# Weight loads moved to ScalarE's queue, a conversion and three copies moved in the start-up, and identity products added between its transposes

## The chip, the cores and the metric

One core of a Trainium2 chip runs the whole kernel. The metric is the device time of one execution in microseconds (us). The engines are TensorE (PE; its weight loads are PEld), VectorE (DVE), ScalarE (ACT), GpSimd (POOL) and SyncE (SP), whose queue issues DMA transfers.

## The reference

```python
def _attn_ref(q, k, v):                      # (4, 8, 576, 64), float32
    scores = scale * np.matmul(q, k.transpose(0, 1, 3, 2))
    rel = pos[:, None] - pos[None, :]
    mask = (rel >= 0) & (rel < 64)
    scores = np.where(mask, scores, -1000000000.0)
    attn = softmax(scores)                   # max taken off, sum + 1e-9
    return np.matmul(attn, v)

def _moe_ref(x, w_gate, w_val, w_out, rms_g):   # (2304, 512), d_ff 1536
    xn = x / sqrt(mean(x * x) + 1e-06) * rms_g
    g = xn @ w_gate
    silu = g * (1.0 / (1.0 + np.exp(-g)))
    return silu * (xn @ w_val) @ w_out

def _moe2_ref(x, w_in, w_out):               # d_ff 2048
    h = x @ w_in
    return (h * (1.0 / (1.0 + np.exp(-1.702 * h)))) @ w_out
```

The three run one after the other. The weights come as 64-bit floats.

## The kernel before

The 2304 tokens are cut into tiles of 128 (index `m`) and blocks of three tiles (384 tokens, index `j`). Attention makes a tile of x from q, k and v; the first MLP goes over all blocks twice (`ps_i`), with six of its twelve slices `f` of 128 columns each time; the second MLP goes over all blocks once.

**Weights.** A pair is two slices of 512 KB, for instance gate and value of one `f`, or two slices of `w_out`; `w_order` lists 34 pairs, and the first block needs pairs 0 to 8 (0: gate and value of slice 0; 1: of slice 1; 2: output of slices 0 and 1; and so on in threes). `w_load` issues a pair's two transfers on SP's queue into one of three `st` buffers. `w_step` converts: two ScalarE operations on `st` (L144, L145), then three VectorE operations that leave a 24-bit value in `m` (L146, L147, L150), of which there is one buffer. `w_half`, called at the start of the next step, casts the high part on ScalarE (L128) and takes the rest on VectorE (L129); from then on products may use the pair. An `st` buffer is free again after L150, and the load of pair i+3 goes into the buffer of pair i.

**Start-up** (tiles 0 to 2, `starting[0]`). For each tile: transposes of k and q, S (L271), masking with a row maximum (L289), exponentials (L301), scaling by the reciprocal sum (L311 to L313), all of it for two halves `e` of four heads. The p of each half is transposed by four TensorE operations into a bank ps_t (L321) and copied to SBUF (`to_sbuf`, L233); then PV (L336), a copy to `xraw` (L344), squares (L353), sums by products with ones (L367), a power on POOL, a product that spreads it (L373), and the scaling of x by it and by `g_sb` (L377). `split_x` casts x to `xh` (L385, L387) and takes `xl` (L389). The products of the first block (`proj`, L396) start there.

**Order.** The program names engines and queues; a scheduler that ranks instructions by a simulated timeline orders each engine's instructions, and each engine and each queue then works strictly in its order, waiting on semaphores. `tc.issue_after(x)` ranks what follows behind instruction x. `hold[0]` is such an instruction for the conversions L144 and L145: in the start-up the last exponential, then the last cast of `split_x`. Attention for later blocks and the conversions are spread over slots (three per `f`) of the MLP blocks; in block 0 there is a `w_step` in every second slot, in the others of that pass one in nine.

Of the kernel before, what the change touches and what calls it, by code (L numbers as in the profile page):

```python
# [8 lines left out]
F32 = mybir.dt.float32  # L9
# [13 lines left out]
def window_attention__gated_mlp__mlp_kernel(  # L23
# [13 lines left out]
    nc = tc.nc  # L37
# [8 lines left out]
    NHP = H // 2  # L46
# [5 lines left out]
    T0 = TB  # L52
# [7 lines left out]
    acc_p = ctx.enter_context(tc.tile_pool(name="acc", bufs=1, space=PSUM))  # L60
# [6 lines left out]
    ident = const.tile([128, 128], F32, name="ident")  # L67
# [5 lines left out]
    QT0 = at.tile([128, NHP, 128], F32, name="QT")  # L73
# [25 lines left out]
    w_next = [0, 0]  # L99
# [3 lines left out]
    def w_src(kind, f):  # L103
        c = slice(f * 128, (f + 1) * 128)
        if kind in "gvh":
            w = {"g": w_gate, "v": w_val, "h": w_in2}[kind]
            return w[:, c].bitcast(I32).rearrange("(k p) f -> p k f", p=128)
        return {"o": w_out, "p": w_out2}[kind][c, :].bitcast(I32)

    def w_load(limit):  # L110
        while w_next[0] < min(limit, n_w):
            pair = w_order[w_next[0]]
            w_next[0] += 1
            st = stp.tile([128, 2, 1024], I32, tag="st", name="st")
            for e, (kind, f) in enumerate(pair):
                dst = st[:, e, :].rearrange("p (k f) -> p k f", k=KC) if kind in "gvh" else st[:, e, :]
                nc.sync.dma_start(out=dst, in_=w_src(kind, f))
            staged.append(st)

    def after(ins):  # L120
        return tc.issue_after(ins) if ins is not None else nullcontext()

    def w_half():
        if not half:
            return
        pair, w24 = half.pop()
        w = wp.tile([128, 2, 1024], F32R, tag="w", name="w")
        nc.scalar.copy(w[:, 0, :], w24.bitcast(F32))  # L128
        nc.vector.tensor_tensor(w[:, 1, :], w24.bitcast(F32), w[:, 0, :].bitcast(F32), ALU.subtract)  # L129
        for e, key in enumerate(pair):  # L130
            weights[key] = w[:, :, e * 512:(e + 1) * 512]

    def w_step(limit):
        w_half()
        if w_next[1] >= min(limit, n_w):
            return
        w_load(w_next[1] + 1)
        pair = w_order[w_next[1]]
        w_next[1] += 1
        st = staged.pop(0).rearrange("p e (f two) -> p (e f) two", two=2)  # L140
        lo, hi = st[:, :, 0], st[:, :, 1]
        m = tmp.tile([128, 1024], I32, tag="tmp", name="m")
        with after(hold[0]):
            nc.scalar.mul(hi.bitcast(F32), hi.bitcast(F32), 2.0 ** -112)  # L144
            nc.scalar.activation(lo, lo.bitcast(U32), AF.Copy, scale=2.0 ** -29)  # L145
        nc.vector.tensor_scalar(m.bitcast(U32), hi.bitcast(U32), 3, None, ALU.logical_shift_left)  # L146
        nc.vector.scalar_tensor_tensor(  # L147
            m.bitcast(U32), hi.bitcast(U32), 0x80000000, m.bitcast(U32), ALU.bitwise_and, ALU.bitwise_or
        )
        nc.vector.tensor_tensor(m, m, lo, ALU.add)  # L150
        half.append((pair, m))
        w_load(w_next[1] + 2)


    NLD = 4
# [57 lines left out]
    hold = [None]  # L213
    starting = [True]
    ps_turn = {}

    def att_bank(kind):
        shape = [128, 512]
        if not starting[0]:
            return atp.tile(shape, F32, tag="att", name="ps_" + kind)  # L220
        ps_turn[kind] = i = ps_turn.get(kind, -1) + 1
        if kind in "kq":
            return acc_p.tile(shape, F32, tag="acc" + "23"[kind == "q"], name="ps_" + kind)
        if kind == "r":
            return acc_p.tile(shape, F32, tag="acc" + "012"[i % 3], name="ps_" + kind)
        if kind == "s":
            return acc_p.tile(shape, F32, tag="acc" + "01"[i % 2], name="ps_" + kind)
        if kind == "v":
            return mm_p.tile(shape, F32, tag="gv"[i % 2], name="ps_" + kind)
        return atp.tile(shape, F32, tag="att", name="ps_" + kind)  # L230

    def to_sbuf(dst, src):
        nc.scalar.copy(dst, src)  # L233

    def att_Tk(m):
        t = ld_tile["k", m]
# [17 lines left out]
        released(("q", m))  # L254

    p_tiles = {}
    last_exp = [None]
    last_pt = [None]
    pt_tiles = {}

    def key_blocks(n):
        return slice(0, 4, 3) if n % 4 == 0 else slice((n - 1) % 4, (n - 1) % 4 + 2)

    def att_S(m):
        QT = qts[m]
        banks = [att_bank("s") for _ in range(2)]
        prev = last_pt[0] if not starting[0] else None
        for hp in range(NHP):
            for g, e in ((0, 0), (0, 1), (1, 0), (1, 1)):
                with after(prev):  # L270
                    prev = nc.tensor.matmul(  # L271
                        banks[e][64 * g:64 * g + 64, hp * 128:(hp + 1) * 128],
                        QT[64 * e:64 * e + 64, hp, 64 * g:64 * g + 64],
                        KT[64 * e:64 * e + 64, hp, key_blocks(2 * m + g), :],
                        start=True,
                        stop=True,
                    ).ins
        first = next((g for g in range(2) if (2 * m + g) % GPB == 0), None)
        mask = masks[:, MASKS.index(((m + 1) % 2, first))].rearrange("p a b -> p (a b)")
        sm = at.tile([128, 3, 2 * NHP], F32, tag="sm", name="sm", bufs=6)  # L280
        if starting[0] and m > 0:
            p = [part_tile().rearrange("p (h t) -> p h t", h=NHP) for _ in range(2)]
        else:
            pp = at.tile([128, 2 * NHP, 128], F32, tag="p", name="p", bufs=1)
            p = [pp[:, e * NHP:(e + 1) * NHP, :] for e in range(2)]
        for e in range(2):
            for hp in range(NHP):
                i = e * NHP + hp
                nc.vector.tensor_tensor_reduce(  # L289
                    p[e][:, hp, :],  # L290
                    banks[e][:, hp * 128:(hp + 1) * 128],
                    mask,
                    op0=ALU.add,
                    op1=ALU.min,
                    scale=-0.125,
                    scalar=3e38,
                    accum_out=sm[:, 0, i:i + 1],
                )
            for hp in range(NHP):
                i = e * NHP + hp  # L300
                last_exp[0] = nc.scalar.activation(  # L301
                    p[e][:, hp, :],
                    p[e][:, hp, :],
                    AF.Exp,
                    bias=sm[:, 0, i:i + 1],
                    scale=-1.0,
                    accum_out=sm[:, 1, i:i + 1],
                ).ins
        for lo, n, pe in [(0, NHP, p[0]), (NHP, NHP, p[1])] if starting[0] else [(0, 2 * NHP, pp)]:
            r = sm[:, 2, lo:lo + n]  # L310
            nc.vector.tensor_scalar(r, sm[:, 1, lo:lo + n], SUM_EPS, None, ALU.add)  # L311
            nc.vector.reciprocal(r, r)
            nc.vector.tensor_tensor(pe, pe, r.unsqueeze(2).to_broadcast([128, n, 128]), ALU.mult)  # L313
        p_tiles[m] = p

    def att_PT(m):
        for e in range(2):
            p = p_tiles[m][e]
            ps = att_bank("t")
            for hp in range(NHP):  # L320
                last_pt[0] = nc.tensor.transpose(ps[:, hp * 128:(hp + 1) * 128], p[:, hp, :], ident).ins  # L321
            if starting[0] and m > 0:
                pt = part_tile().rearrange("p (h t) -> p h t", h=NHP)
            else:
                pt = at.tile([128, NHP, 128], F32, tag="pt", name="pt", bufs=2)
            to_sbuf(pt, ps.rearrange("p (h t) -> p h t", h=NHP))
            pt_tiles[m, e] = pt

    def att_PV(m, x, c0):
# [116 lines left out]
    m = TB // 128  # L446
    for fn in (att_Tk, att_Tq):
        at_slot(0, 0, lambda m=m, fn=fn: held(fn, m))
    for b in range(1, NB):
        for i in range(TB // 128):  # L450
            m = b * TB // 128 + i
# [6 lines left out]
            h = b - 1  # L458
# [12 lines left out]
    if True:  # L471
# [1 line left out]
        nc.sync.dma_start(out=g_sb, in_=rms_g.rearrange("(k p) -> p k", p=128))  # L473
        make_identity(nc, ident)
        nc.vector.memset(QT0, 0.0)
        ps_warm = att_bank("v")
        for _ in range(10):
            nc.tensor.matmul(ps_warm[:, 0:128], QT0[:, 0, :], QT0[:, 0, :], start=True, stop=True)
        nc.vector.memset(KT[:, :, 3, :], 0.0)
        nc.vector.memset(ones, 1.0 / DM)  # L480
        nc.vector.memset(mhalf, -0.5)
# [20 lines left out]
        for m in range(T0 // 128):  # L502
            att_S(m)
            if m + 1 < T0 // 128:
                att_Tk(m + 1)
                att_Tq(m + 1)
        hold[0] = last_exp[0]
        w_step(1)
        for m in range(T0 // 128):
            att_PT(m)  # L510
            att_PV(m, x, m * 128)
            s4 = rms_sq(x, m * 128, sq)
            pe_hold = rms_scale(x, sq, m * 128, (m + 1) * 128, s4)
# [181 lines left out]
```

## Time and profile before

| | |
|---|---|
| median of 3 runs | 1029.68 us (1028.36 to 1031.18) |
| profiled execution | 1027.21 us, span 1025.4 us from first to last instruction |
| mean granted TensorE clock | 0.979 of full |
| busy, share of the span | PE 96%, PEld 89%, DVE 50%, ACT 40%, POOL 1% |
| chain that ended last | PE 83%, DVE 6%, ACT 5%, DMA 4% |

Times in the rows below count from the start of the span. A busy share is an average over the whole span; the table by stages in the rows tells the stages apart. A line L128 is line 128 of the kernel. A trace counts most 32-bit products as two records, since TensorE takes them in two passes; a transpose is one.

### The profile page before, as it was taken

The numbers are of one execution on the slowest core, as the hardware profiler recorded it, in microseconds if no ns is written. First come the engines' busy times: TensorE is split into PE (matmuls) and PEld (weight loads), VectorE is DVE, ScalarE is ACT, GpSimd is POOL, SyncE is SP. The second block draws the span as 40 slices with busy tenths as digits, with TensorE's granted clock in tenths as the row PEclk, the third lists the DMA queues.
The fourth block names the chain that finished last, engine by engine and source line by source line (L and its number), as shares of the span: only waits on it lengthen the run. The fifth ranks groups of instructions, "written<-read, shape, count | busy, mean of one in ns | idle before, by whom it ended". The sixth has DMA issues, their size and how long they took to land.

```text
span 1025.4 us, 15454 instructions
## 1 busy us (share of the span) xinstructions
PE 987.4 (96%) x6158; PEld 917.1 (89%) x6158; DVE 517.4 (50%) x1132; ACT 408.7 (40%) x884; POOL 12.2 (1%) x39
## 2 busy tenths in 40 slices
PE   7888999999989999999999999999999999999997
PEld 5877798988989899999999998998989989999996
DVE  5597756655575655656543688332232322322222
ACT  7586654654554333333332365222222222322222
POOL 2000000000000000000000000000000000000000
PEclk9698999999999999999999999999999999999999
DMA  9648644444361512423411352010010000000000
GB/s 233 184 124 212 181 102 133 101 86 135 83 186 42 196 66 87 165 72 122 157 72 63 113 171 77 1 62 1 1 62 1 32 31 1 31 1 1 32 1 31
DMA packets 113320, 88.43 MB, mean 86 GB/s; under 512 B 77664, under 2 KB 104288, under 8 KB 113248
## 3 DMA queue, kind: packets, MB, share of 16 engines
q1 hardware_dynamic: 113248, 87.44, 29.4%
q8 instruction: 48, 0.79, 0.3%
q14 instruction: 24, 0.20, 0.1%
HBM read 68.55 MB, written 18.87 MB: 85 GB/s over the span
## 4 chain that ended last, share of the span: by engine, by line
PE 83%; DVE 6%; ACT 5%; DMA 4%; issue 1%; SPq 0%; POOL 0%; DVEq 0%; ACTq 0%
PE acc L622 20%; PE psh L396 19%; PE acc L531 13%; PE psg L396 12%; PE psv L396 12%; PE ps_s L271 2%; PE ps_v L336 2%; ACT p L301 1%; PE ps_t L321 1%; DMA st<-in_moe_w_in_dram 1%; DMA st<-in_moe_w_val_dram 1%; DVE xraw L377 1%; ACT st L145 1%; DMA o<-x2s 1%; PE ps_r L367 1%
## 5 line engine op out<-in xcount | busy, mean ns | idle before, releaser
L638 DVE TENSOR_TENSOR a<-a,psh 128x384 f32<-128x384 f32 x96 | 53.0, 553 | 201.9 <-ACT a L637 201.9
L396 PE MATMUL psh<-x2h,w 128*128 128x384 f32 x768 | 153.3, 339 | 0.9 <-DVE a L638 0.6
L622 PE MATMUL acc<-w,gh 128*128 128x512 f32 x576 | 152.9, 397 | 0.0
L396 PEld LDWEIGHTS psh<-x2h,w 128*128 128x128 f32 x768 | 137.2, 188 | 4.3 <-DVE a L638 0.9
L637 ACT ACTIVATE a<-psh 128x384 f32<-128x384 f32 x96 | 47.0, 491 | 220.4 <-PE psh L396 217.2
L622 PEld LDWEIGHTS acc<-w,gh 128*128 128x128 f32 x576 | 107.1, 188 | 18.5
L531 PE MATMUL acc<-ah,w 128*128 128x384 f32 x576 | 117.6, 344 | 3.6 <-ACT w L128 3.3
L531 PEld LDWEIGHTS acc<-ah,w 128*128 128x128 f32 x576 | 103.5, 190 | 4.9 <-ACT w L128 3.7
L565 DVE SCALAR_TENSOR_TENSOR a<-a,psg 128x384 f32<-128x384 f32 x72 | 39.7, 552 | 115.5 <-ACT a L562 115.3
L396 PE MATMUL psh<-x2l,w 128*128 128x384 f32 x384 | 86.2, 338 | 0.0
L622 PE MATMUL acc<-w,gl 128*128 128x512 f32 x288 | 85.1, 396 | 0.0
L642 DVE TENSOR_TENSOR gl<-a,gh 128x384 fp32r<-128x384 f32 x96 | 53.4, 557 | 50.5 <-ACT gh L641 42.7
L562 ACT ACTIVATE a<-psg 128x384 f32<-128x384 f32 x72 | 35.1, 487 | 107.7 <-PE psg L396 107.7
L396 PEld LDWEIGHTS psh<-x2l,w 128*128 128x128 f32 x384 | 69.9, 188 | 5.9
L641 ACT CAST gh<-a 128x384 fp32r<-128x384 f32 x96 | 49.3, 513 | 62.5 <-DVE a L638 49.7
L396 PE MATMUL psg<-xh,w 128*128 128x384 f32 x288 | 65.3, 357 | 6.4 <-DVE a L565 2.6
L622 PEld LDWEIGHTS acc<-w,gl 128*128 128x128 f32 x288 | 54.2, 189 | 12.5
L531 PE MATMUL acc<-al,w 128*128 128x384 f32 x288 | 64.8, 343 | 0.0
L572 ACT CAST ah<-a 128x384 fp32r<-128x384 f32 x72 | 36.8, 511 | 70.1 <-DVE a L569 69.9
L396 PE MATMUL psv<-xh,w 128*128 128x384 f32 x288 | 62.9, 346 | 0.0
L396 PEld LDWEIGHTS psg<-xh,w 128*128 128x128 f32 x288 | 51.3, 193 | 11.4 <-DVE a L565 3.6
L301 ACT ACTIVATE p<-p,sm 128x128 f32<-128x128 f32 x128 | 49.6, 391 | 23.6 <-DVE sm L289 23.6
(104 smaller groups left out, 1433.6 us busy)
## 6 DMA issues: line engine op xcount, KB each, us to landing
st<-in_moe_w_out_dram SPq DMA_DIRECT2D x28, 512.0 KB, 4.3
o<-x2s SPq DMA_DIRECT2D x48, 192.0 KB, 3.4
st<-in_moe_w_in_dram SPq DMA_DIRECT2D x16, 512.0 KB, 5.0
st<-in_moe_w_gate_dram SPq DMA_DIRECT2D x12, 512.0 KB, 4.9
st<-in_moe_w_val_dram SPq DMA_DIRECT2D x12, 512.0 KB, 5.6
qkv<-in_v_dram SPq DMA_DIRECT2D x20, 256.0 KB, 4.2
x<-xraw SPq DMA_DIRECT2D x6, 768.0 KB, 4.7
xr<-x SPq DMA_DIRECT2D x6, 768.0 KB, 4.4
```

What stands on the lines that cost most here:

```text
L271: prev = nc.tensor.matmul(banks[e][64 * g:64 * g + 64, hp * 128:(hp + 1) * 128], QT[64 * e:64 * e + 64, hp, 64 * g:64 * g + 64], KT[64 * e ...
L301: last_exp[0] = nc.scalar.activation(p[e][:, hp, :], p[e][:, hp, :], AF.Exp, bias=sm[:, 0, i:i + 1], scale=-1.0, accum_out=sm[:, 1, i:i + ...
L396: nc.tensor.matmul(ps[:, :T], w[:, wi, c * 128:(c + 1) * 128], xx[:, c, :T], start=(i == 0), stop=(i == 3 * KC - 1),)
L531: nc.tensor.matmul(acc[c][:, :T], w[:, wi, c * 128:(c + 1) * 128], aa, start=(f == f_lo and pi == 0), stop=(f == f_hi - 1 and pi == 2),)
L562: tanh = nc.scalar.activation(a, psg[:, :T], AF.Tanh, scale=0.5).ins
L565: nc.vector.scalar_tensor_tensor(a, a, 1.0, psg[:, :T], ALU.add, ALU.mult)
L572: nc.scalar.copy(ah, a)
L622: nc.tensor.matmul(acc[c], (gh, gh, gl)[pi][:, c * 128:(c + 1) * 128], w[:, (0, 1, 0)[pi], :], start=(f == 0 and pi == 0), stop=(f == NF2 ...
L637: nc.scalar.activation(a[:, :T], psh[:, :T], AF.Sigmoid, scale=1.702)
L638: nc.vector.tensor_tensor(a[:, :T], a[:, :T], psh[:, :T], ALU.mult)
L641: nc.scalar.copy(gh[:, :T], a[:, :T])
L642: nc.vector.tensor_tensor(gl[:, :T], a[:, :T], gh[:, :T].bitcast(F32), ALU.subtract)
```

## The change

Five edits. (1) Every load of a pair behind the first three (31 pairs, 62 transfers) is issued on ScalarE's queue behind the cast L128 of the pair three before it, no longer on SP's. (2) The first `w_step`, which converts pair 0, is called behind the transposes of the last start-up tile, and its conversions are ranked behind the copy of that tile's first p half. (3) In the start-up the copy of each second p half runs on VectorE. (4) Behind each group of four p transposes in the start-up come five products of the identity with itself into a bank `ps_warm` that nothing reads. (5) A bank is renamed.

```diff
-    def w_load(limit):
+    def w_load(limit, queue=None):
+        queue = queue or nc.sync
         while w_next[0] < min(limit, n_w):
...
-                nc.sync.dma_start(out=dst, in_=w_src(kind, f))
+                queue.dma_start(out=dst, in_=w_src(kind, f))
             staged.append(st)
...
         w = wp.tile([128, 2, 1024], F32R, tag="w", name="w")
-        nc.scalar.copy(w[:, 0, :], w24.bitcast(F32))
+        cast = nc.scalar.copy(w[:, 0, :], w24.bitcast(F32)).ins
+        with tc.issue_after(cast):
+            w_load(w_next[0] + 1, nc.scalar)
...
         if w_next[1] >= min(limit, n_w):
             return
-        w_load(w_next[1] + 1)
...
         half.append((pair, m))
-        w_load(w_next[1] + 2)
...
-    def to_sbuf(dst, src):
-        nc.scalar.copy(dst, src)
+    def to_sbuf(dst, src, other=False):
+        if other:
+            return nc.vector.tensor_copy(dst, src)
+        return nc.scalar.copy(dst, src)
...
                 last_pt[0] = nc.tensor.transpose(ps[:, hp * 128:(hp + 1) * 128], p[:, hp, :], ident).ins
+            if starting[0]:
+                with tc.issue_after(last_pt[0]):
+                    for _ in range(5):
+                        nc.tensor.matmul(ps_warm[0][:, 0:128], ident, ident, start=True, stop=True)
...
-            to_sbuf(pt, ps.rearrange("p (h t) -> p h t", h=NHP))
+            copy = to_sbuf(pt, ps.rearrange("p (h t) -> p h t", h=NHP), starting[0] and e == 1)
+            if e == 0:
+                last_copy[0] = copy.ins
             pt_tiles[m, e] = pt
...
-        hold[0] = last_exp[0]
-        w_step(1)
+        ps_warm = [acc_p.tile([128, 512], F32, tag="acc3", name="ps_warm")]
         for m in range(T0 // 128):
             att_PT(m)
+            if m == T0 // 128 - 1:
+                hold[0] = last_copy[0]
+                w_step(1)
             att_PV(m, x, m * 128)
```

What the scheduler makes of it, at three places. First ScalarE in the start-up, from the exponentials of tile 1 on; `pt` and `quad<-ps_t` are copies of p halves, `st` the conversions of pair 0, `xraw` a tile of x. Before:

```order
L301 ACTIVATE quad,sm<-quad,sm 128x128 x8
L233 COPY pt<-ps_t 128x512
L301 ACTIVATE quad,sm<-quad,sm 128x128 x4
L233 COPY quad<-ps_t 128x512
L301 ACTIVATE quad,sm<-quad,sm 128x128 x3
L144 ACTIVATE st<-st 128x1024
L145 ACTIVATE st<-st 128x1024
L344 COPY xraw<-ps_v 128x4x128
L233 COPY quad<-ps_t 128x512 x2
L353 ACTIVATE s_417<-xraw 128x512
L128 CAST w<-m 128x1024
```

With the change (line numbers are the changed kernel's; L146 and L147 are the two conversions there, L129 the cast, L118 the loads):

```order
L304 ACTIVATE quad,sm<-quad,sm 128x128 x15
L236 COPY quad<-ps_t 128x512
L353 COPY xraw<-ps_v 128x4x128
L362 ACTIVATE s_422<-xraw 128x512
L236 COPY quad<-ps_t 128x512
L146 ACTIVATE st<-st 128x1024
L147 ACTIVATE st<-st 128x1024
L353 COPY xraw<-ps_v 128x4x128
L362 ACTIVATE s_478<-xraw 128x512
L129 CAST w<-m 128x1024
L118 DMA st<-in_moe_w_gate_dram 128x4x256
L118 DMA st<-in_moe_w_val_dram 128x4x256
```

The exponentials stand together, three copies are gone, the conversions have moved behind tile 0's squares and tile 2's first copy, and pair 3's transfers stand behind the cast.

Second TensorE in the same stretch, from the second half of tile 0's transposes on (`ps_r<-ones` are tile sums). Before:

```order
L321 MATMUL ps_t<-ident,p 128x128 x4
L321 MATMUL ps_t<-ident,quad 128x128 x4
L336 MATMUL ps_v<-pt,quad 64x64 x15
L321 MATMUL ps_t<-ident,quad 128x128 x4
L336 MATMUL ps_v<-quad 64x64
L321 MATMUL ps_t<-ident,quad 128x128 x4
L336 MATMUL ps_v<-quad 64x64 x15
L321 MATMUL ps_t<-ident,quad 128x128 x4
L336 MATMUL ps_v<-quad 64x64
L367 MATMUL ps_r<-ones,s_417 128x1 x4
```

With the change:

```order
L324 MATMUL ps_t<-ident,p 128x128 x4
L328 MATMUL ps_warm<-ident 128x128 x5
L324 MATMUL ps_t<-ident,quad 128x128 x4
L328 MATMUL ps_warm<-ident 128x128 x5
L345 MATMUL ps_v<-pt,quad 64x64 x15
L324 MATMUL ps_t<-ident,quad 128x128 x4
L328 MATMUL ps_warm<-ident 128x128 x5
L345 MATMUL ps_v<-quad 64x64
L324 MATMUL ps_t<-ident,quad 128x128 x4
L328 MATMUL ps_warm<-ident 128x128 x5
L376 MATMUL ps_r<-ones,s_422 128x1 x4
L345 MATMUL ps_v<-quad 64x64 x15
```

Groups of five stand behind every four transposes, and tile 0's sums have moved ahead of tile 1's PV.

Third ScalarE in the first block, from the conversions of pair 3 on (`a<-psg` is the activation, `ah` its cast). Before:

```order
L144 ACTIVATE st<-st 128x1024
L145 ACTIVATE st<-st 128x1024
L233 COPY QT<-ps_q 128x512
L562 ACTIVATE a<-psg 128x384
L128 CAST w<-m 128x1024
L572 CAST ah<-a 128x384
L144 ACTIVATE st<-st 128x1024
L145 ACTIVATE st<-st 128x1024
L301 ACTIVATE p,sm<-p,sm 128x128 x8
L562 ACTIVATE a<-psg 128x384
L128 CAST w<-m 128x1024
L233 COPY KT<-ps_k 128x4x128
```

With the change:

```order
L146 ACTIVATE st<-st 128x1024
L147 ACTIVATE st<-st 128x1024
L236 COPY QT<-ps_q 128x512
L129 CAST w<-m 128x1024
L118 DMA st<-in_moe_w_gate_dram 128x4x256
L118 DMA st<-in_moe_w_val_dram 128x4x256
L573 ACTIVATE a<-psg 128x384
L146 ACTIVATE st<-st 128x1024
L147 ACTIVATE st<-st 128x1024
L304 ACTIVATE p,sm<-p,sm 128x128 x6
L573 ACTIVATE a<-psg 128x384
L583 CAST ah<-a 128x384
```

Pair 4's transfers stand behind the cast of pair 1 and close ahead of pair 4's own conversions.

## Rows read from the trace of the kernel before

**Rows 1.** Table by stage: us, busy by engine (records), granted clock, DMA share, GB/s.

```profile
0.00:41.00 41.00, 32.40 (x299) 27.59 (x299) 20.55 (x92) 24.09 (x73) 7.89 (x34) 0.75 0.94 203
41.00:118.00 77.00, 65.01 (x522) 58.02 (x520) 62.70 (x146) 56.69 (x129) 0.86 (x1) 0.91 0.66 180
118.00:700.00 582.00, 570.44 (x3757) 543.99 (x3757) 340.47 (x724) 245.09 (x520) 3.42 (x4) 0.99 0.34 104
```

**Rows 2.** Chain of waits, 14 to 42 us: start, us on the chain, what.

```profile
15.31 2.71 ACT quad L301 x14
...
22.80 1.02 ACT st L144
23.82 1.02 ACT st L145
...
25.84 1.97 PE ps_v L336 x30
...
39.68 1.12 DVE xraw L377 x4
```

**Rows 3.** Table by slices of 5 us, columns as in group 1.

```profile
15.00:20.00 5.00, 3.05 (x52) 2.22 (x52) 4.00 (x24) 4.36 (x21) 0.00 (x0) 1.00 1.07 279
20.00:25.00 5.00, 3.43 (x37) 2.46 (x32) 3.80 (x16) 5.00 (x17) 0.00 (x0) 0.56 1.17 305
...
35.00:40.00 5.00, 3.90 (x16) 3.52 (x17) 2.36 (x11) 0.63 (x1) 1.11 (x2) 0.50 0.01 2
...
45.00:50.00 5.00, 3.54 (x46) 2.98 (x45) 2.60 (x5) 4.65 (x7) 0.00 (x0) 1.00 0.68 192
```

**Rows 4.** Timeline of the start-up: start, us, engine, line, what.

```profile
1.44 4.34 PEld L478 LDWEIGHTS ps_v<-QT 128*128 128x128 f32 x20 [1.44 <-DVE QT L475]
...
16.92 0.69 DVE L313 TENSOR_TENSOR quad<-quad,sm 128x512 f32<-128x512 f32 x1
...
18.35 0.26 DVE L289 CUSTOM_DVE_ANT_0 quad<-ps_s,masks 128x128 f32<-128x128 f32 x1
...
19.05 0.56 ACT L233 COPY pt<-ps_t 128x512 f32<-128x512 f32 x1
...
19.67 1.26 PE L336 MATMUL ps_v<-pt,quad 128*64 128x64 f32 x30 [1.28 <-ACT pt L233]
...
25.95 3.60 SPq L473 DMA_DIRECT2D g_sb<-in_moe_rms_g_dram  x1
```

**Rows 5.** One line's instructions: durations in ns (min/median/max), first and last start.

```profile
L346 DVE COPY xraw<-ps_v x12: 682/684/692, 125.9 to 329.3; 128x512 f32<-128x512 f32 x12
```

**Rows 6.** DMA issues from 0 to 120 us: KB, median us to landing.

```profile
g_sb<-in_moe_rms_g_dram SPq DMA_DIRECT2D x1, 2.0 KB, 7.1
```

**Rows 7.** L144 from 40 to 47 us, on ScalarE's queue (ACTq) and on the engine.

```profile
L144 ACTq EVENT_SEMAPHORE  x3: 17/17/17, 40.6 to 40.8; - x3
L144 ACT ACTIVATE st<-st x3: 1130/1168/1184, 41.4 to 45.6; 128x1024 f32<-128x1024 f32 x3
```

**Rows 8.** Chain of waits in the first block.

```profile
46.88 4.68 DMA st<-in_moe_w_val_dram
...
75.55 5.80 DMA st<-in_moe_w_val_dram
```

**Rows 9.** TensorE's waits, 40 to 120 us: total, times, longest.

```profile
PE ps_s L271 <- ACT pt L233: 4.3, 1, 4.3
```

**Rows 10.** Timeline of SP's queue and ScalarE around the load of pair 7.

```profile
72.18 2.65 SPq L206 DMA_DIRECT2D qkv<-in_v_dram  x4
74.94 0.56 SPq L117 DMA_DIRECT2D st<-in_moe_w_gate_dram  x1
75.55 0.50 SPq L117 DMA_DIRECT2D st<-in_moe_w_val_dram  x1
...
79.86 1.71 SPq L117 DMA_DIRECT2D st<-in_moe_w_out_dram  x2
...
81.44 1.10 ACT L144 ACTIVATE st<-st 128x1024 f32<-128x1024 f32 x1 [3.36 <-DMA st<-in_moe_w_val_dram]
```

More of the change, by code (lines that the diff above doesn't have):

```diff
@@ L256, in window_attention__gated_mlp__mlp_kernel @@
     p_tiles = {}
-    last_exp = [None]
+    last_copy = [None]
     last_pt = [None]
@@ L300, in att_S @@
                 i = e * NHP + hp
-                last_exp[0] = nc.scalar.activation(
+                nc.scalar.activation(
                     p[e][:, hp, :],
@@ L307, in att_S @@
                     accum_out=sm[:, 1, i:i + 1],
-                ).ins
+                )
         for lo, n, pe in [(0, NHP, p[0]), (NHP, NHP, p[1])] if starting[0] else [(0, 2 * NHP, pp)]:
@@ L475, in window_attention__gated_mlp__mlp_kernel @@
         nc.vector.memset(QT0, 0.0)
-        ps_warm = att_bank("v")
+        ps_first = att_bank("v")
         for _ in range(10):
-            nc.tensor.matmul(ps_warm[:, 0:128], QT0[:, 0, :], QT0[:, 0, :], start=True, stop=True)
+            nc.tensor.matmul(ps_first[:, 0:128], QT0[:, 0, :], QT0[:, 0, :], start=True, stop=True)
         nc.vector.memset(KT[:, :, 3, :], 0.0)
```

## Prediction

> **What bounds the kernel now.** First the table by stages. In the start-up (0 to 41 us, attention of the first three tiles) TensorE works 32.4 of 41 us at a mean granted clock of 0.75; in the first MLP block (41 to 118 us) it is busy 65.0 of 77 us and VectorE 62.7; from 118 to 700 us it works 98% of the time at 0.99 [rows 1]. All that the change touches after 118 us lies beside a full TensorE, so its price is decided before that.
>
> Next the chain of waits through the start-up [rows 2]. To 22.8 us it runs over ScalarE (exponentials, 14 records in 2.71 us, so 0.39 us each with the reading of its sum). Then stand 2.04 us of the first weight pair's two conversions (L144, L145, 22.80 to 24.84), ahead of the copies that TensorE waits for. From 25.84 on it runs over TensorE, whose products are slow: 30 records of PV take 1.97 us there and 1.26 us at 19.67 [rows 2, 4]. Why, the clock says: 1.00 from 15 to 20 us (TensorE busy 3.05 of 5), 0.56 in the next slice, 0.50 up to 40 [rows 3], so the lower of the two levels, 1.2 GHz, from about 20.6 us on, after TensorE had worked little.
>
> In the first block the reader is to see that weights come late: the chain holds two stretches of 4.68 and 5.80 us of weight transfer [rows 8], TensorE's longest wait is 4.3 us for a pt copy [rows 9], and that copy stood on ScalarE behind an L144 that waited 3.36 us for weights; these were issued at 74.94, behind four loads of v that held SP's queue for 2.65 us [rows 10].
>
> **The change part by part.**
>
> *First pair moved.* The two conversions leave the chain at 22.80: −2.04 us there. They now run behind tile 2's first p copy, where ScalarE waits for TensorE anyway. The pair is needed only at 41 us; even late it is ready by about 32.
>
> *Copies shared.* Three of six p copies go to VectorE. A 128x512 copy out of PSUM takes VectorE 0.68 us [rows 5], ScalarE 0.56 [rows 4]. VectorE's order also changes: tile 2's mask products (L289) come right behind tile 1's first scaling, which ends at 16.92+0.69 = 17.6, and not at 18.35 [rows 4]. Tile 1's exponentials end at 15.31+2.71 = 18.0 [rows 2], so tile 2's start at 18.1 and run without a copy between them: 8 x 0.39 ends them at 21.2, not 22.8. The copy of tile 0's second half waits on VectorE for eight mask products (0.21 apart) until 19.5 and ends at 20.2; ScalarE's ended at 19.6. That costs 0.6 us at the first PV.
>
> *Idle products.* Thirty products, each two passes as in the warm-up, whose 20 passes took 4.34 us at the start, 0.217 each [rows 4]. I take that for the lower level, since the slow stretch has the same ratio to the fast one; at the upper level it is half, 0.108. A group of five is then 1.1 us, or 2.2 us at the lower clock. Two groups fall into TensorE's gaps before 19 us; four lie on its path: +4.3 us at the upper, +8.7 us at the lower clock. No row shows identity products between transposes. For the upper clock speaks how the gaps close: 15 to 20 us had 3.05 us of work, two groups make it about 5, and a stretch with 3.54 of 5 kept 1.00 at 45 to 50 us [rows 3]. I take the upper clock up to 31 us.
>
> Now the walk, at the upper clock. PV of tile 0 from 20.2 to 21.4; four transposes (0.65) and a group (1.1) to 23.1; tile 2's first transposes (p scaled at 22.1) and a group to 25.0; sums of tile 0 (eight passes, 0.9) to 25.9; PV of tile 1 to 27.0; last transposes and group to 28.7; PV of tile 2 with tile 1's sums between to 31.0; copy and square on ScalarE to 32.2; last sums to 33.1. Behind that VectorE scales three tiles at 1.1 us each (the 1.12 us of four [rows 2]), and here a new wait stands: g_sb, issued at 25.95 [rows 4], lands 7.1 us later [rows 6], at 33.05. Scaling runs from there, through the last tile's sum and power on VectorE and POOL, to 36.7, with its first quarter done at 35.9. Before, the last tile's first quarter was done at 39.96, one of four after 39.68 [rows 2]. **Start-up: −4.1 us** (−5 if g_sb lands earlier; +4.2 if the clock falls as before, by the same walk at 1.2 GHz).
>
> *Loads on ScalarE's queue.* 31 pairs, 62 issues, move. On SP the two of pair 7 took 0.56 and 0.50 us [rows 10]. The question is when ScalarE's queue issues: behind the cast (L128) in program order. In the trace its queue runs ahead of its engine: three wait records of L144 pass at 40.6 to 40.8 us, while the engine starts those L144 at 41.4 to 45.6 [rows 7]. So I let a load go as soon as the cast's data is there (L150 done) and the queue has come that far, and let its 1.1 us per pair hide under the cast, a pass over as many columns as the conversions' 1.02 us [rows 2], and the work queued before it. A load then starts when SP would have started it, except: pair 7 goes at about 73.5 and not 74.94, no longer behind the v loads; pair 8, which SP issued at 79.86 [rows 10], goes only at about 83.5 since the cast of pair 5 is the next thing in ScalarE's order behind pair 7's conversion. (Times in this paragraph are on the clock of before; the start-up's gain comes off all.) Step by step along ScalarE's new order: pair 4's landing stays at 51.6; casts of pairs 2 and 3 come 1.4 and 0.9 us later (other copies stand ahead), pair 4's cast 2.6 us later since pair 6's conversion now stands ahead of eight exponentials. Pair 7 lands 2.7 us earlier, which gives that back: cast 5 stands at −0.4. Pair 8 lands 2 us late: cast 6 at +1.0, cast 8 at +1.6 (VectorE has four mask products ahead). The block's last output products hide 1.4 of that, as PV of tile 5 now runs ahead of them and not between; so the norm of the next block is ready 1 to 2 us earlier behind them. I take **−1.0 us** for the first block, between −3.5 and +2. Later loads are hidden: TensorE works 98% [rows 1] and each pair has a stretch of nine slots.
>
> The Trainium skill, "DMA: Bandwidth & Descriptors", section "Issuing engines are not separate DMA queues", speaks against this part: transfers issued by any engine share the same 16 DMA engines, so a second queue saves no more than the sequencer's issue time. By this rule of the Trainium skill the part would bring the time that SP stood in front of pair 7 at most, and the sum would be between −4.1 and −5.5 us, which lies within the forecast's own range below; no run here shows two queues yet.
>
> **Sum.** −4.1 −1.0 = −5.1 us against the profiled execution's 1027.2 us (span 1025.4): 1022.1. The median of the three runs, 1029.7, lies 2.5 us above that execution; against it I forecast **1024.6 us**. A measurement of this kernel tells about 0.3% (3.1 us) from no change.
>
> **The rivals.**
>
> *Loads held by the cast itself.* If ScalarE's queue issues a load only when the engine starts the cast, or later, each of pairs 4 to 8 starts 1 to 4 us later than I have it, and L144, which stands close behind its own load in the new order (pair 6's directly), stalls ScalarE with exponentials behind it. The same walk with issue at the cast's start gives: cast 2 at +3.0, cast 4 at +5.5, cast 6 at +5.7, block end +5.7. Sum −4.1+5.7 = +1.6: 1031.3. For it: L144 already waited 3.36 us on weights [rows 10]. Against it: [rows 7]. The Trainium skill, "Perfetto Trace Analysis", section on the per-instruction lifecycle: the issuing sequencer is taken from the end of its wait to the end of descriptor generation, and free only then; it would cost this much only where the cast doesn't cover it, and no run here shows it on ScalarE.
>
> *The clock falls all the same* (the slower side). The place is 20 us; it decides whether the groups before suffice. Then each of four groups costs 2.2 us on the path: start-up +4.2, with −1.0 from the block 1032.9. For it: the clock fell within a stretch that was 3 of 5 busy. Against it: two added groups fill that stretch.
>
> *Gain swallowed.* The start-up ends earlier, but the first block is paced by something not moved with it (SP's loads of k, q, v, landed by fixed traffic): 1029.7. For it: SP's queue waits long behind buffers. Against it: those buffers are freed by work that moves too, and the conversions there wait for the last split.
>
> *More.* With loads no longer behind SP's queue both long stretches of [rows 8] shrink by 2 us or so: −4.1−5 = −9.1, 1020.6.
>
> **How the numbers follow.** Forecast 0.55 (its own range 1021.5 to 1027.5), held loads 0.17, clock 0.10, swallowed 0.08, more 0.10. The range 1019.5 to 1031.8 takes in the forecast, the swallowed case, the held loads and the larger gain, and leaves out the slow clock and the tails of both sides. Faster by over 0.3%: 0.85 of the forecast and all of the larger gain, 0.57. Slower: the clock case, 0.10. Within: the rest, 0.33.
>
> **What the profile of the changed kernel would show.** The first xh cast near 36 us (behind 39.96 before); clock 1.00 from 20 to 31 us, with groups of ten passes at 1.1 us; the two conversions of pair 0 behind 24 us. ScalarE's queue with issues of about 0.5 us that begin when L150 ends; if they begin with the cast, the first rival holds, and L144 waits for weights at every pair from 4 to 8. Wrong I would be most simply if the first block is longer than 77 us by over 4: then the queue's order costs more than the start-up gives.

## The result, and the profile after

The changed kernel takes 1038.14 us (median of 5, 1037.15 to 1042.94) against 1029.51 us before on the same chip: ratio 1.0105, 95% interval 1.0077 to 1.0132. It is slower by about 1%; 1024.6 us had been predicted. The profiled execution has a span of 1035.9 us (before 1025.4). A ratio, here and below, is taken from all executions and not from the two medians; one of the six of e6, 1599.1 us at a granted clock of 0.56, is left out of its figures.

The table by stages of the changed kernel, columns as in [rows 1]:

```profile
0.00:41.00 41.00, 33.88 (x362) 30.30 (x363) 22.85 (x97) 24.04 (x71) 8.81 (x34) 0.92 0.97 205
41.00:118.00 77.00, 62.60 (x514) 55.68 (x512) 60.46 (x141) 54.08 (x125) 0.86 (x1) 0.93 0.68 179
118.00:700.00 582.00, 567.48 (x3711) 542.57 (x3712) 339.78 (x721) 243.85 (x516) 3.42 (x4) 0.98 0.35 104
```

It hides the answer as [rows 1] did: 98% busy behind 118 us has become 97.5%, and the clock 0.98. Marks along the program (starts in the profiled executions, us) show the place. Each store of x starts within 1 us of the second `xh` cast of the next block; the last two marks are loads of x (`xr`) for the second pass and for the second MLP. The last three columns are experiments below: e3 mends the order at the first four block ends, e9 that and `g_sb`, e8 is e9 without edit 1.

| | before | after | e3 | e9 | e8 |
|---|---|---|---|---|---|
| first `xh` cast | 40.06 | 38.91 | 39.77 | 35.77 | 35.77 |
| store of x, block 1 | 117.97 | 118.37 | 119.60 | 113.63 | 113.22 |
| block 2 | 176.82 | 179.68 | 177.46 | 170.86 | 170.46 |
| block 3 | 234.81 | 238.86 | 236.50 | 229.89 | 229.51 |
| block 4 | 293.32 | 297.77 | 294.63 | 288.09 | 287.94 |
| block 5 | 342.88 | 350.67 | 346.46 | 339.91 | 339.56 |
| third load of xr, for the second pass | 381.54 | 392.12 | 387.66 | 381.15 | 378.11 |
| a load of xr, for the second MLP | 679.42 | 689.88 | 684.92 | 678.35 | 675.05 |

The start-up gains 1.15 us and not 4.1, the first block gives that back, and then the kernel loses at every block end up to 392 us, 10 us in all. From there to the end nothing more.

**Start-up.** The same slices of 5 us as [rows 3], after: the clock stays up to 30 us and longer.

```profile
15.00:20.00 5.00, 5.00 (x65) 4.47 (x64) 4.47 (x30) 5.00 (x26) 0.00 (x0) 1.00 1.00 270
20.00:25.00 5.00, 5.00 (x65) 4.62 (x64) 3.12 (x9) 3.72 (x11) 0.00 (x0) 1.00 1.12 305
25.00:30.00 5.00, 5.00 (x78) 4.54 (x76) 3.73 (x5) 3.51 (x5) 1.46 (x1) 1.00 1.14 273
30.00:35.00 5.00, 2.88 (x30) 2.53 (x28) 1.29 (x2) 1.65 (x3) 0.56 (x1) 0.93 1.14 227
35.00:40.00 5.00, 2.37 (x11) 2.37 (x12) 3.68 (x15) 1.09 (x3) 0.55 (x1) 0.50 0.08 24
```

TensorE's timeline follows the walk of the prediction: first PV at 20.24 (forecast 20.2), a group of idle products 1.28 us (forecast 1.1), the last sums done at 33.9 (forecast 33.1).

```profile
20.24 1.15 PE L345 MATMUL ps_v<-pt,quad 128*64 128x64 f32 x30
...
21.80 1.28 PE L328 MATMUL ps_warm<-ident 128*128 128x128 f32 x10
...
32.83 1.05 PE L376 MATMUL ps_r<-ones,s 128*128 128x1 f32 x8 [1.33 <-ACT s L362]
```

But the chain behind it hangs on `g_sb`, 8.81 us on its way (7.1 in [rows 6]):

```profile
26.92 8.81 DMA g_sb<-in_moe_rms_g_dram
35.80 0.23 issue
36.03 0.86 DVE xraw L386 x3
...
38.91 0.51 ACT xh L396
```

**First block.** ScalarE's queue (ACTq) issues pair 4's loads 1.5 us ahead of the engine's cast (L129), as forecast from [rows 7]:

```profile
45.39 0.37 ACTq L118 DMA_DIRECT2D st<-in_moe_w_gate_dram  x1
...
45.80 0.52 ACTq L118 DMA_DIRECT2D st<-in_moe_w_val_dram  x1
...
46.86 1.11 ACT L129 CAST w<-m 128x1024 fp32r<-128x1024 f32 x1
```

Pairs 5 to 7 are issued 0.4 to 2.3 us ahead of their casts too, pair 8 together with its cast (84.95 and 84.94). The conversions waited longer for their weights all the same; lines of ScalarE's waits from 41 to 118 us (in total, times, longest), before and then after:

```profile
ACT st L144 <- DMA st<-in_moe_w_val_dram: 4.6, 2, 3.4
ACT st L144 <- DMA st<-in_moe_w_out_dram: 0.9, 1, 0.9
```

```profile
ACT st L146 <- DMA st<-in_moe_w_val_dram: 7.3, 3, 3.4
ACT st L146 <- DMA st<-in_moe_w_out_dram: 2.9, 2, 2.6
```

**Block ends.** What TensorE waited for between 118 and 360 us (in total, times, longest); first the line of before, then that of after:

```profile
PE psg L396 <- ACT xh L387: 2.3, 3, 0.8
```

```profile
PE psg L405 <- ACT xh L396: 6.4, 3, 2.4
```

Why the casts are late, ScalarE's timeline shows at the end of the second block. `x2s` is the eviction of a finished output bank (L606, after L617); ScalarE does two of a block's four. There are two buffers, so its second must wait until the store of its first has landed. Before:

```profile
173.36 0.51 ACT L387 CAST xh<-xraw 128x384 fp32r<-128x384 f32 x1 [0.68 <-DVE xraw L377]
175.88 0.49 ACT L606 ACTIVATE x2s<-acc 128x384 f32<-128x384 f32 x1 [2.01 <-DMA o<-x2s]
176.27 0.50 ACT L387 CAST xh<-xraw 128x384 fp32r<-128x384 f32 x1
```

After:

```profile
176.77 0.59 ACT L236 COPY pt<-ps_t 128x512 f32<-128x512 f32 x1 [0.75 <-PE ps_t L324]
178.75 0.49 ACT L617 ACTIVATE x2s<-acc 128x384 f32<-128x384 f32 x1 [1.39 <-DMA o<-x2s]
179.13 0.92 ACT L396 CAST xh<-xraw 128x384 fp32r<-128x384 f32 x2
```

Before, one cast ran ahead of the waiting `x2s`, and the next block's products began on it. After, both stand behind. The Trainium skill, "Perfetto Trace Analysis", section "Tensor Engine Instruction (MATMUL, LD_WEIGHTS)", notes that ScalarE (ACT) is a strict first-in-first-out engine; the trace agrees, both casts follow at once, at 179.13, on an `x2s` that had waited 1.39 us. At the first block end a copy of p stood behind it as well (117.71, on an `x2s` that had waited 1.56 us), and TensorE waited for that:

```profile
118.35 0.43 PE L274 MATMUL ps_s<-KT,QT 64*64 64x128 f32 x2 [1.79 <-ACT pt L236]
```

TensorE's longer gap then costs a second time. Windows of 16 us around the five block ends, columns as in [rows 1], before:

```profile
112.00:128.00 16.00, 13.89 (x135) 11.74 (x134) 11.39 (x39) 9.21 (x30) 0.86 (x1) 1.00 0.74 198
168.00:184.00 16.00, 13.83 (x125) 11.66 (x126) 12.07 (x38) 8.54 (x26) 0.85 (x1) 0.89 0.70 210
228.00:244.00 16.00, 12.67 (x116) 10.78 (x115) 11.92 (x37) 8.46 (x26) 0.85 (x1) 0.89 0.72 217
286.00:302.00 16.00, 13.21 (x127) 11.31 (x127) 12.52 (x39) 9.32 (x28) 0.85 (x1) 1.00 0.64 208
340.00:356.00 16.00, 13.64 (x75) 12.60 (x74) 12.71 (x26) 5.66 (x11) 0.00 (x0) 1.00 0.88 312
```

After:

```profile
112.00:128.00 16.00, 13.60 (x86) 11.19 (x84) 8.28 (x32) 6.73 (x24) 0.86 (x1) 0.79 0.58 151
173.00:189.00 16.00, 12.80 (x119) 11.11 (x118) 12.44 (x38) 8.40 (x27) 0.85 (x1) 0.89 0.63 195
232.00:248.00 16.00, 12.49 (x117) 10.55 (x116) 11.40 (x36) 8.14 (x26) 0.85 (x1) 0.89 0.63 195
290.00:306.00 16.00, 12.79 (x86) 10.95 (x84) 12.42 (x38) 7.96 (x25) 0.85 (x1) 0.79 0.66 210
349.00:365.00 16.00, 12.77 (x61) 11.72 (x60) 11.30 (x24) 5.45 (x11) 0.00 (x0) 0.89 0.90 299
```

TensorE stands idle 15.6 us in these windows, before 12.8. The clock's shortfall, 16 us times what is missing to 1.00, adds to 12.0 us, before to 3.5. So 2.8 us more of idle time and 8.5 us more lost to the lower clock, together 11.3, stand against the 11.7 us by which the stretch from the first cast to the third load of xr (381.54, after 392.12) has grown.

At the fifth block end the last block of the first pass begins. Its two casts on ScalarE come early there, and what is late is the `tanh` (L562, after L573). Before, and then after:

```profile
347.97 0.49 ACT L562 ACTIVATE a<-psg 128x384 f32<-128x384 f32 x1 [2.25 <-PE psg L396]
348.36 1.04 ACT L128 CAST w<-m 128x1024 fp32r<-128x1024 f32 x1
351.24 0.49 ACT L606 ACTIVATE x2s<-acc 128x384 f32<-128x384 f32 x1 [1.84 <-DMA o<-x2s]
```

```profile
356.64 0.49 ACT L617 ACTIVATE x2s<-acc 128x384 f32<-128x384 f32 x1 [2.86 <-DMA o<-x2s]
...
357.03 0.48 ACT L573 ACTIVATE a<-psg 128x384 f32<-128x384 f32 x1
```

### The profile page after: what moved, and what is told of

Its sections match the earlier page's. It is cut to its first block, busy times and chain, and to the rows that moved or that the text cites. A ratio compares the mean times of both kernels' runs of the same rounds, so it can differ in the third digit from the quotient of the medians.

```text
span 1035.9 us, 15522 instructions
## 1 busy us (share of the span) xinstructions
PE 993.9 (96%) x6218; PEld 925.0 (89%) x6218; DVE 519.5 (50%) x1135; ACT 407.5 (39%) x881; POOL 13.1 (1%) x39
## 4 chain that ended last, share of the span: by engine, by line
PE 83%; DMA 7%; ACT 4%; SPq 2%; DVE 2%; issue 1%; ACTq 0%; POOL 0%; DVEq 0%
PE acc L633 19%; PE psh L405 19%; PE psg L405 14%; PE psv L405 13%; PE acc L542 12%; DMA o<-x2s 2%; DMA st<-in_moe_w_out_dram 2%; PE ps_s L274 2%; SPq L207 2%; PE ps_v L345 1%; ACT st L146 1%; DMA st<-in_moe_w_val_dram 1%; DMA st<-in_moe_w_in_dram 1%; DMA g_sb<-in_moe_rms_g_dram 1%; SPq L118 1%
## 5 line engine op out<-in xcount | busy, mean ns | idle before, releaser
L405 PE MATMUL psg<-xh,w 128*128 128x384 f32 x288 | 69.6, 376 | 13.4 <-ACT xh L396 6.4
L573 ACT ACTIVATE a<-psg 128x384 f32<-128x384 f32 x72 | 35.3, 491 | 109.0 <-PE psg L405 108.8
L405 PEld LDWEIGHTS psg<-xh,w 128*128 128x128 f32 x288 | 55.0, 207 | 18.9 <-ACT xh L396 7.4
```

Of the source, the lines that this page charges most:

```text
L405: nc.tensor.matmul(ps[:, :T], w[:, wi, c * 128:(c + 1) * 128], xx[:, c, :T], start=(i == 0), stop=(i == 3 * KC - 1),)
L573: tanh = nc.scalar.activation(a, psg[:, :T], AF.Tanh, scale=0.5).ins
```

## The experiments

Theory S: the scheduler, given the loads on ScalarE, put the waiting `x2s` ahead of the `xh` casts (and of a `tanh`), and the clock falls in the gap. Theory Q: the load issues themselves hold ScalarE up. Theory U: edits 2 to 5 lose it. Beside these, `g_sb`'s late landing.

**e1: edit 1 alone, e2: edits 2 to 5 without it.** The diffs are the parts of the change.

> The kernel before with edit 1 alone: loads on ScalarE's queue, start-up untouched. Theory S (order at the block ends: ScalarE's second x2s, which waits for a store to land, stands ahead of the xh casts, and TensorE's clock falls in the gap): this kernel has that order at three of four block ends, so +5 to +7 us against the kernel before, 1035 to 1037. Theory Q (the two issues of a weight pair, about 0.5 us each, stand on ScalarE between the cast and the pt copies at the ends of the second to fourth block, whatever the x2s does): all of the loss and the start-up's lost gain too, +9 to +11, 1039 to 1041. Theory U (the start-up's edits cause it): same as before, 1028 to 1031.

> Edits 2 to 5 without edit 1: the loads stay on SP. ScalarE's order at the second to fourth block end is that of the kernel before; at the first the second x2s still stands ahead of both xh casts. Theory S: start-up -1.2 us, first block end +2, so 1029 to 1032. Theory Q: start-up -1.2 and nothing behind it, 1027 to 1029.5. Theory U: 1036 to 1039, as the changed kernel.

Measured: e1 1036.98 us, ratio 1.0077 (1.0050 to 1.0105); e2 1026.33 us, ratio 0.9972 (0.9956 to 0.9988). Theory U falls: edits 2 to 5 gain 0.28%, and edit 1 costs 1.3% on top of them. e1 is where S had it. e2 is better than either theory said, since its first cast stands at 36.96: with pair 3 on SP's queue `g_sb` lands after 6.6 us. The first block end, where the `x2s` stands ahead of the casts without edit 1 too, lost what S had priced at 2 us: the second block takes 61.67 us from store to store, 58.85 before.

**e3: the second x2s behind the casts.**

```diff
-                        split_x(x, nxh, nxl, T)
+                        x_cast = split_x(x, nxh, nxl, T)
...
-                        nc.scalar.mul(st, acc[c][:, :T], 0.5)
+                        with after(x_cast if c == 2 and not end else None):
+                            nc.scalar.mul(st, acc[c][:, :T], 0.5)
```

> The changed kernel with the second x2s on ScalarE ranked behind the last xh cast at the four block ends of the first pass; the loads' issues stay where they are. Theory S: 5 to 8 us come back, 1030 to 1033, and TensorE's wait on xh shrinks from up to 6.4 us to about 3. Theory Q: under 2 us come back, 1036 to 1039.

Measured: 1032.42 us, ratio 1.0028 (1.0011 to 1.0045), so 0.77% or 8 us come back with no load moved. At the second block end ScalarE now shows

```profile
175.89 0.51 ACT L396 CAST xh<-xraw 128x384 fp32r<-128x384 f32 x1 [0.73 <-DVE xraw L386]
176.94 0.51 ACT L396 CAST xh<-xraw 128x384 fp32r<-128x384 f32 x1 [0.54 <-DVE xraw L386]
177.36 0.48 ACT L618 ACTIVATE x2s<-acc 128x384 f32<-128x384 f32 x1
```

and TensorE's waits on `xh` are back to what they were before (2.3 us):

```profile
PE psg L405 <- ACT xh L396: 2.4, 3, 0.8
```

The load issues stand where they stood, and the traces of the two kernels have every engine's instructions in the same order but for the moved `x2s` (and, on SP's queue, its store, now behind that of x). So Q's range is missed, and the order that S names is shown as the cause of most of the loss. The clock's part is shown only in part: in windows of 16 us around e3's five block ends (from 112, 171, 230, 288 and 345 us) TensorE stands idle 12.2 us, as little as before, but the clock still falls at four of them, and its shortfall is 8.6 us (after 12.0, before 3.5). The two profiles show 5.3 of these 8 us (first cast to third load of xr, 353.2 and 347.9 us).

**e4: g_sb first, e6: pair 3 on SP.** Both are edits of the changed kernel.

```diff
+        nc.scalar.dma_start(out=g_sb, in_=rms_g.rearrange("(k p) -> p k", p=128))
         load_some()
-        nc.sync.dma_start(out=g_sb, in_=rms_g.rearrange("(k p) -> p k", p=128))
```

```diff
-            w_load(w_next[0] + 1, nc.scalar)
+            w_load(w_next[0] + 1, nc.scalar if w_next[0] > 3 else nc.sync)
```

> The changed kernel with g_sb's transfer issued first, on ScalarE's queue, and not behind the q, k, v and weight loads on SP's. If g_sb's landing (35.73 us) is what holds the scaling of x, the first xh cast goes from 38.9 to 36 us and the whole kernel gains 2.5 to 3 us, 1035 to 1036. Rival: what the start-up gains is lost again at the first block's end, since that is paced by transfers: 1037.5 to 1038.5.

> The changed kernel with the load of pair 3 alone back on SP's queue, where it stands behind g_sb. Theory: the 1 MB of pair 3, issued at 29.4 us on ScalarE's queue, fills the DMA engines ahead of the 2 KB of g_sb, issued at 26.9; then g_sb lands at 33.5 to 34 and not at 35.73, the first xh cast stands at about 37 and not 38.91, and the time falls by 1.5 to 2 us, to 1036 to 1037. Rival: g_sb is late for the q, k and v loads ahead of it; then nothing changes: 1037.5 to 1039.

Measured: e4 1035.39 us, ratio 1.0062 (1.0039 to 1.0084); e6 1036.06 us, ratio 1.0075 (1.0057 to 1.0093). The first cast stands at 35.99 in e4. In e6 the chain shows

```profile
26.71 6.05 DMA g_sb<-in_moe_rms_g_dram
...
35.94 0.51 ACT xh L396
```

Pair 3's 1 MB, issued 2.5 us behind `g_sb` on the other queue (ACTq, 29.39), kept these 2 KB waiting for 2.8 us; behind it on the same queue (30.16 in e6) it did not. All else stands in the same order in the two kernels, so that moving this load delayed `g_sb` is shown. The runs can't tell whether the other queue did it or the earlier time: on SP's queue pair 3 goes only when the issue of `g_sb` has ended (3.4 us in e6).

**e5: only pairs 3 to 11 on ScalarE's queue** (in the line of e6, `nc.scalar if w_next[0] < 12 else nc.sync`).

> The changed kernel with ScalarE's queue for the loads of pairs 3 to 11 only; all later ones go back to SP's queue. ScalarE's order at the second to fourth block end is then again that of the kernel without edit 1. If the later loads cost by what they do to the order at those block ends: 6 to 8 us back, 1030 to 1032, with a first block as long as the changed kernel's. If the loads of the first block are the cost: 1036 to 1038. If the loads cost nothing but in the start-up (g_sb late): 1028 to 1029.

Measured: 1029.65 us, ratio 1.0020 (1.0000 to 1.0041). 0.85% come back, by moving loads that TensorE never waited for: in the changed kernel it has no wait on a weight from 118 us on. `g_sb` was late here too (10.7 us), and the first cast at 41.25, in a profiled execution of 1034.02 us; the twelve executions range from 1024.1 to 1035.3.

**e7 and e8: loads on SP, g_sb first, and (e8) the casts ahead of x2s.** Edits 2 to 5 with the diffs of e4 and e3.

> Edits 2 to 5 without edit 1, and g_sb's transfer issued first on ScalarE's queue. Without edit 1 the first xh cast stood at 36.96; with g_sb there in time at about 36.0: 1025 to 1025.8, a gain of 0.5 to 1.3 us on it. Rival: the block end after it swallows that, 1026.3.

> The same, with the second x2s ranked behind the last xh cast at the four block ends, which without edit 1 changes the first block end most. By theory S the clock stays up at 118 to 125 us and 1.5 to 2.5 us more come back: 1022.5 to 1024.5. By theory Q nothing: 1025 to 1026.

Measured: e7 1024.95 us, ratio 0.9972 (0.9960 to 0.9984), the same ratio as e2: an early `g_sb` brings nothing that can be measured where it was in time or nearly so. e8 1022.52 us, ratio 0.9948 (0.9935 to 0.9960), the fastest version: by 0.5% faster than before. Between e7 and e8 the order at the block ends differs, and the second block's length falls from 59.39 to 57.24 us (store to store), which S had said.

**e9 and e10: edit 1 again, with both repairs** (e9: the changed kernel with the diffs of e3 and e4; e10: with that of e5 as well).

> The changed kernel with both repairs: g_sb's transfer first on ScalarE's queue, and the second x2s behind the xh casts. The same without edit 1 took 1022.5 us, so this is the price of edit 1 when neither the late g_sb nor the x2s order can cost. If those two were all: 1022 to 1024. If the load issues on ScalarE cost by themselves (in the first block, which was 1 to 1.5 us longer with them, and in front of the pt copies at the block ends): 1026 to 1029.

> The same two repairs, with ScalarE's queue for pairs 3 to 11 only. If the loads on ScalarE's queue gain anything in the first block, as the prediction's term of -1.0 had it: 1021 to 1022. If they lose there what the blocks' lengths so far say: 1023.5 to 1025. If the loss of edit 1 lies at the later block ends, this stands below the kernel with all loads on that queue by 2 us or more.

Measured: e9 1027.94 us, ratio 1.0009 (0.9995 to 1.0022); e10 1024.20 us, ratio 0.9965 (0.9949 to 0.9980). So S and `g_sb` together make up 1.0%, and edit 1 still costs 0.6% against e8. The columns e9 and e8 of the table stand level, within 0.5 us, to 339.91 and part at the fifth block end, by 2.7 us. e10, with the first block's loads on ScalarE's queue and the others on SP's, stands 0.44% below e9 and 0.17% above e8, which is within the noise: most of what edit 1 still costs in e9 comes with the loads of pairs 12 on.

**e11: e8 without the idle products** (the loop of five is taken out).

> The kernel of edits 2 and 3 with both repairs and all loads on SP's queue, but without the idle identity products (edit 4). If these hold the clock, as the prediction said: it falls to 0.50 near 20 us, the first xh cast goes from 35.8 to about 38 to 39 us, and the time from 1022.5 to 1024.5 to 1026. If the clock would have stayed up without them: the groups on TensorE's path are only cost, the first cast stands at 33 to 34.5 and the time is 1020 to 1022.

Measured: 1026.90 us, ratio 0.9994 (0.9981 to 1.0007), 0.46% above e8. The clock falls as before the change:

```profile
20.00:25.00 5.00, 3.83 (x38) 3.27 (x39) 3.79 (x14) 3.78 (x15) 0.00 (x0) 0.51 1.15 302
25.00:30.00 5.00, 5.00 (x46) 4.87 (x46) 2.65 (x4) 3.57 (x5) 0.95 (x1) 0.50 1.14 268
```

and the first cast stands at 38.69, 2.9 us behind e8.

**e12: the diff of e3 on the kernel before, e14: that of e4 on it.**

> The kernel before with one thing changed: the second x2s ranked behind both xh casts, which moves it past one cast at four block ends. Theory S: each of these block ends is shorter by the 0.2 to 0.9 us that ScalarE waited for the store, and by the clock where it fell (172 to 180 and 228 to 236 us): 1 to 4 us faster, 1024 to 1027. Theory Q, or if order at block ends matters only with the loads among it: same, 1027.5 to 1029.

> The kernel before with g_sb's transfer first, on ScalarE's queue. There g_sb landed at 33.05 us and the first scaling came behind slower work, so nothing should move: 1026.5 to 1028.5, first xh cast at 39.5 to 40.1. If g_sb held it too: first cast up to 1.5 us earlier and 1025.5 to 1026.5.

Measured: e12 1027.46 us, ratio 1.0000 (0.9987 to 1.0013); e14 1028.21 us, ratio 1.0006 (0.9989 to 1.0024). For e12 S had said 1 to 4 us, and that was wrong: where one cast already ran ahead of the waiting `x2s`, moving the second there too changed nothing that TensorE waited for (on `xh` 2.3 us in three waits from 118 to 360 us, as before). That the harm begins where both stand behind is what e3 and e12 suggest together. e14's time is as said. Its first cast, 38.88, is earlier than said, but so is e12's, 38.93, with `g_sb` as before: `g_sb` held only the start-up that had become faster.

**e13: e9 with the load of pair 19 alone on SP** (`nc.scalar if w_next[0] != 19 else nc.sync`). On ScalarE this takes away two issues and turns the order at the fifth block end round; up to there every engine's order stands as it was.

> The changed kernel with both repairs, and the load of one pair, number 19, back on SP's queue; the other 30 stay on ScalarE's. With that the second x2s at the end of the fifth block falls behind the next block's tanh again. If that order is the rest of what edit 1 costs: 3 us back, 1024.5 to 1025.5, and xr's transfer at about 345 us (346.80 before it). If the issues themselves cost: 1027 to 1028.5.

Measured: 1026.80 us, ratio 0.9987 (0.9972 to 1.0002), 0.2% below e9, little more than the noise and between the two expectations. The order is that of before again:

```profile
348.88 0.49 ACT L573 ACTIVATE a<-psg 128x384 f32<-128x384 f32 x1 [2.32 <-PE psg L405]
349.27 1.04 ACT L129 CAST w<-m 128x1024 fp32r<-128x1024 f32 x1
...
351.95 0.49 ACT L618 ACTIVATE x2s<-acc 128x384 f32<-128x384 f32 x1 [1.65 <-DMA o<-x2s]
```

and from the fifth store of x to the third load of xr it takes 38.62 us, as in e8 (38.55), where e9 took 41.24: the 2.6 us of that place are shown. That the load of xr which the expectation names, the second, stands at 349.30 and not near 345 comes from the blocks ahead. The fifth store of x is 3.9 us behind e9's; 1.8 us of this are the first block's, 78.79 us from store to store here, 76.97 in e9, with the same instructions in the same order on every engine.

## Why the prediction was wrong

**The step that failed** is the first paragraph's "All that the change touches after 118 us lies beside a full TensorE, so its price is decided before that." The 98% of [rows 1] is an average. Around each block end TensorE was busy 12.7 to 13.9 of 16 us before the change, waiting in part for ScalarE's copies and casts, and twice the clock was already down to 0.89 in such a window. The sum had a zero for these five places; they cost 10.2 of the 10.5 us between the two profiles, for the most part because the `x2s` that waits for a store came to stand ahead of the casts (e3 gives 8 us back) and of a `tanh` (e13, 2.6 us). That the loads are hidden was right (no wait on weights behind 118 us), and beside the point: what they moved was ScalarE's order. Of that order the prediction had read the start-up and the first block only.

**A term mis-sized**: the start-up's −4.1 measured −1.15. The walk held to about 33 us; `g_sb` was to land at 33.05 by the 7.1 us of [rows 6], and landed at 35.73. The prediction named this wait as new, but took for it a landing time measured with nothing on another queue. With `g_sb` in time the first cast stands at 35.8 to 36.0 (e4, e8), where the prediction had 35.9. The 1.15 itself is little more than the spread of single profiles: e12 and e14, with the start-up's engine work as before, have their first casts at 38.93 and 38.88, before had 40.06.

**A term not borne out**: −1.0 in the first block. From first to second store of x the block takes 76.6 to 78.7 us in the seven profiles with loads on SP, 77.3 on average, and 75.5 to 78.9 in the nine with loads on ScalarE, 77.7. No gain shows. The rule of the Trainium skill that the prediction cited ("DMA: Bandwidth & Descriptors", "Issuing engines are not separate DMA queues"), that transfers of all queues share the engines and a second queue saves only the issue, left room for little or no gain; the lengths, 77.3 and 77.7 us, agree.

**Right**: the idle products hold the clock at 1.00 and are worth 0.46% (e11), so the slow-clock rival falls; its direction, slower, came true by another mechanism. The price of a group, 1.1 us against a measured 1.28, came near by luck in part: the 0.217 us of a warm-up pass were taken for the lower clock, but the profile of before has the granted clock at 1.00 from 1.44 to 6.00 us, and why those passes took twice as long stays open.

**Half right**: the queue runs ahead of its engine, as forecast, and loads held by the cast are not the cause of the loss: e3 gives most of it back with the loads where they stood. But the other sign of that rival came: L146 waited for weights at every pair from 4 to 8, 10.2 us in all against L144's 5.5 before. The first block was 1.5 us longer than before in these two profiles, not 5.7, and that is inside the spread of its length. The rival of the swallowed gain falls: e4's first cast is 2.9 us ahead of the changed kernel's, and its first store of x still 2.65 us.

**Still open**: e13 and e8 differ by 0.39%, with ScalarE's order of `x2s`, casts and `tanh` alike at all block ends; other orders still differ, TensorE's products in the fourth block among them, and no run tests what these cost. In the two profiles 2.2 of 4.9 us lie in the first block, but there e9, e10 and e13, whose orders are alike on every engine, took 77.0, 75.6 and 78.8 us, so single profiles can't place it. Open too is why the clock still falls at four of e3's block ends.

## What to carry to other kernels

Moving an instruction to an in-order engine's queue moves everything that the scheduler ranks beside it: compare the order over the whole program, and look for an instruction with a long wait that has come to stand ahead of one on the path. Where TensorE is nearly full on average, price each change at the ends of its blocks, in windows of a few us: there lie its gaps, and a slightly longer one can cost several us more at the lower clock (first block end: 2.1 us idle before, 2.4 after, mean clock 1.00 and 0.79). A small transfer that the path hangs on belongs well ahead of the large ones: being issued first was not enough here.

## What the runs showed of the hardware

The 2 KB of `g_sb` landed after 6.0 to 7.3 us where the next 1 MB was issued behind it on its own queue, 3.4 to 3.7 us later (before, e2, e6, e12); after 8.8 to 10.7 us where that 1 MB was issued on another engine's queue, 0.4 to 2.5 us later (the changed kernel, e1, e3, e5); and after 3.6 to 3.9 us as the first of all (e4, e7 to e11, e13, e14). So a transfer issued later, on another queue, can still hold up one under way.

How long TensorE is idle does not tell by itself whether the clock falls. In the kernel before it stood idle 2.8 of the 16 us around the fourth block end, and the granted clock stayed 1.00; in the changed kernel 2.4 of 16 around the first, 1.79 us of it in one piece ahead of 118.35, and the mean clock was 0.79. Around the second block end it stood idle 2.2 us before and 2.3 in e3, at mean clocks of 0.89 and 0.79.

One and the same first block took 75.6, 77.0 and 78.8 us in three kernels (e10, e9, e13) that differ only behind it.
